# Chunked attention and two feed-forward layers on one core: the first four attention tiles with whole exponentials, a maximum subtracted on TensorE, and a normalisation on GpSimd

## The chip, the core and the metric

The kernel runs on one core of one Trainium2 chip. The metric is device time in microseconds (us) of one execution. Engines are named as the profile names them: PE (TensorE; PEld is its loading of weights), DVE (VectorE), ACT (ScalarE), POOL (GpSimd) and SP (SyncE, here the engine that issues all transfers; SPq is its queue).

## The reference, cut to what matters

```python
def _attn_ref(q, k, v, mem_k, mem_v):        # (4, 8, 768, 64), 8 memory keys
    chunk, left_ctx, right_ctx = (32, 16, 8)
    scale = 1.0 / np.sqrt(D)
    for c in range(S // chunk):
        ...
        scores = scale * np.matmul(q_c, k_full.transpose(0, 1, 3, 2))
        scores = scores - np.max(scores, axis=-1, keepdims=True)
        a = np.exp(scores)
        a = a / (np.sum(a, axis=-1, keepdims=True) + 1e-09)
        out[:, :, c_start:c_end] = np.matmul(a, v_full)
...
h = x @ w_in                                 # x: 3072 tokens x 512; w_in 512 x 2048
g = np.maximum(h, 0.0) + alpha * np.minimum(h, 0.0)
x = g @ w_out                                # layer 1
...
h = x @ w_in2; sp = np.log1p(np.exp(h))      # sp with a cut at 20
out = (h * np.tanh(sp)) @ w_out2             # layer 2
```

Each chunk of 32 queries sees 64 keys: 16 to its left, its own 32, 8 to its right and 8 memory keys. The result, 3072 tokens of 512 numbers, goes through two feed-forward layers. The weights come as float64.

## The kernel before, in words

The tokens are cut into 24 attention tiles of 128 tokens (`T`, 0 to 23) and six blocks of 512 tokens. Layer 1 goes through w1_in in 16 tiles of 128 columns (`j`), each followed by the product with the w1_out tile of the same number. Every float32 operand is split into a high and a low part (`xh`, `xl`, `wi`, `wo`, `gh`, `gl`), and a product is three matmuls: high by high, high by low, low by high.

Nothing runs in the order in which it is written. Every step is given to `Plan.add` (line 108) with its engine, a planned duration, the buffers that it reads and writes, and for some a due time. `Plan.run` (line 132) then sorts the steps of each engine by due times that it works back from the order of PE's steps, which is the written one, and emits each engine's instructions in that order. On the chip each engine takes its instructions strictly one after another. While PE would have nothing to do at the start, the planner puts in matmuls on a tile of zeros, `busy` (line 1758).

The change touches the first block, tiles 0 to 3 (`T0` is 4), and the first weights:

- `load_qk` (line 612) loads keys and queries of a tile. The queries are then copied by ACT and DVE (`place`, line 638) into a tile `qbd` in which each head's half of the rows is zero outside its own columns, so that one matmul serves two heads. POOL fills the zeros (line 584).
- `load_v` (line 676) loads the values, two rows of 2 KB in each of 96 partitions.
- `gate` (line 604) is a transfer of 4 bytes that reads a tile which has just been loaded or scaled. SP issues transfers in order, so what stands behind a gate is held until that tile is ready. There are five: after the keys of tile 3, the values of tiles 0 and 2, and the scaling of the first two w1_in tiles.
- `scores_of` (line 716) makes a tile's scores, 16 matmuls into one bank of PSUM. `rest` (line 774) adds the softmax: for tiles 0 and 1 a maximum (DVE), eight exponentials with their sums (`exps`, ACT, line 755) and a normalisation (DVE, line 772); for tiles 2 and 3 (`WHOLE`) the maximum is subtracted (DVE, `less`, line 762), one exponential covers the tile (ACT, line 765), and DVE sums (line 768).
- `turn_pe` (line 959) transposes the probabilities on PE in two banks, which ACT or DVE copy out; `values_of` (line 793) multiplies them with the values, and ACT and DVE split the result into `xh` and `xl`.
- `load_raw` (line 332) and `to_f32` (line 352) load a weight tile and make float32 of float64: ACT scales the upper words (line 365), DVE puts the bits together (lines 368 and 371); `split_w` (line 402) splits the result (ACT 404, DVE 407).
- `gemm1` (line 1197) is the product with one tile of w1_in. For the first block, tiles 0 and 1 of w1_in are multiplied in two halves of 256 tokens (line 1795). Their banks are 4 and 5 by turns (line 1200), so the product with the third tile writes the bank that `act1` (line 1226) reads for the first: two ACT reads, lines 1229 and 1230.

The order of the first block's steps on PE is one string (line 1073; s scores, t transposes, v values):

```python
first = "s0 s1 t0 s2 t1 s3 v0 t2 v1 t3 v2 v3"
```

## Time and profile before

| | |
|---|---|
| median of 3 runs | 1034.07 us (1033.57 to 1034.28) |
| the profiled execution: its time | 1034.0 us |
| its span, first to last instruction | 1032.1 us |
| mean granted TensorE clock | 0.998 |
| PE busy | 1020.7 us, 99% of the span |
| PEld busy | 842.1 us, 82% |
| DVE busy | 834.1 us, 81% |
| ACT busy | 641.8 us, 62% |
| POOL busy | 6.9 us, 1% |
| DMA | 242.35 MB, 235 GB/s on average |

The span runs from the first to the last instruction of the core; the execution's own time holds 1.9 us more. Busy times are sums over the whole span, and PE's is modelled, as its matmuls overlap. The chain of waits follows the work that ended last back to its start. Durations of one instruction overlap too: an instruction of DVE with 0.68 us may be followed by the next after 0.60.

### The profile page before, as it was taken

What the parts mean: (1) busy time and instruction counts of PE and PEld (TensorE: products, weight loads), DVE (VectorE), ACT (ScalarE), POOL (GpSimd) and SP (SyncE); (2) the same over time, 40 slices, a digit from 0 to 9 for tenths busy, and PEclk for the clock granted to TensorE, in tenths of its full rate; (3) what the DMA queues carried; (4) which work ended last, traced back from release to release, by engine and by line L of the source; (5) the groups of instructions that cost most, each with busy time, mean ns of one, the idle gap of its engine ahead of it and who ended that gap; (6) DMA issues with size and microseconds to landing.
All of it is one profiled execution on the core that took longest, in us unless ns stands there. A gap on an engine that the chain in (4) does not pass through costs nothing.

```text
span 1032.1 us, 19612 instructions
## 1 busy us (share of the span) xinstructions
PE 1020.7 (99%) x7195; PEld 842.1 (82%) x7197; DVE 834.1 (81%) x1481; ACT 641.8 (62%) x1401; POOL 6.9 (1%) x20
## 2 busy tenths in 40 slices
PE   8999999999999999999999999999999999999997
PEld 6888888888888788888888888888888888888886
DVE  7877688888878889999999969697578777578784
ACT  6899756656665655797977657564444744444630
POOL 2000000000000000000000000000000000000000
PEclk9999999999999999999999999999999999999999
DMA  8977785875687773734878899886778766668766
GB/s 254 318 249 241 245 286 168 258 252 177 223 265 268 243 243 123 255 113 165 296 243 292 296 319 322 306 259 193 227 233 261 218 194 193 192 193 262 209 193 146
DMA packets 133929, 242.35 MB, mean 235 GB/s; under 512 B 12874, under 2 KB 50250, under 8 KB 133834
## 3 DMA queue, kind: packets, MB, share of 16 engines
q1 hardware_dynamic: 131658, 240.05, 73.6%
q10 hardware_dynamic: 2176, 1.05, 0.5%
q8 instruction: 57, 0.93, 0.4%
q14 instruction: 38, 0.31, 0.1%
HBM read 182.33 MB, written 58.72 MB: 234 GB/s over the span
## 4 chain that ended last, share of the span: by engine, by line
PE 97%; DMA 1%; ACT 0%; SPq 0%; issue 0%; DVE 0%; ACTq 0%
PE bank L1522 29%; PE bank L1364 22%; PE bank L1259 17%; PE bank L1210 17%; PE bank L1701 7%; PE bank L927 2%; PE bank L861 1%; DMA wo<-in_w_out_dram 1%; PE bank L1494 1%; DMA wo<-in_kw_dram 1%; PE bank L1758 0%; PE bank L805 0%; PE bank L738 0%; PE bank L998 0%; SPq L635 0%
## 5 line engine op out<-in xcount | busy, mean ns | idle before, releaser
L1210 PE MATMUL bank<-xh,wi 128*128 128x512 f32 (+1 forms) x528 | 170.1, 385 | 0.9 <-ACT rstrip L1230 0.9
L1259 PE MATMUL bank<-gh,wo 128*128 128x512 f32 x512 | 170.3, 392 | 0.2 <-issue 0.2
L1210 PEld LDWEIGHTS bank<-xh,wi 128*128 128x128 f32 x528 | 98.2, 188 | 20.7 <-ACT rstrip L1230 1.1
L1259 PEld LDWEIGHTS bank<-gh,wo 128*128 128x128 f32 x512 | 96.0, 188 | 20.6
L1364 PE MATMUL bank<-wo,wo 128*128 128x512 f32 x438 | 111.1, 389 | 0.0
L1210 PE MATMUL bank<-xl,wi 128*128 128x512 f32 (+1 forms) x264 | 101.1, 383 | 0.0
L1259 PE MATMUL bank<-gl,wo 128*128 128x512 f32 x256 | 99.7, 390 | 0.0
L1364 PEld LDWEIGHTS bank<-wo,wo 128*128 128x128 f32 x438 | 82.2, 188 | 17.0
L1522 PE MATMUL bank<-wi,wo 128*128 128x512 f32 x294 | 73.6, 389 | 0.0
L1229 ACT ACTIVATE rstrip<-bank 128x512 f32<-128x512 f32 x64 | 40.7, 636 | 50.7 <-PE bank L1210 50.4
L1364 PE MATMUL bank<-wo,wi 128*128 128x512 f32 x282 | 71.2, 389 | 0.0
L1522 PEld LDWEIGHTS bank<-wi,wo 128*128 128x128 f32 x294 | 55.2, 188 | 11.4
L1522 PE MATMUL bank<-wi,wi 128*128 128x512 f32 x258 | 64.5, 389 | 0.0
L1222 ACT CAST gh<-rstrip 128x512 fp32r<-128x512 f32 x64 | 42.5, 663 | 35.4 <-PE bank L1259 20.4
L1233 DVE SCALAR_TENSOR_TENSOR rstrip<-rstrip,nalpha 128x512 f32<-128x512 f32 x64 | 47.9, 749 | 19.6 <-ACT rstrip L1230 19.1
L1364 PEld LDWEIGHTS bank<-wo,wi 128*128 128x128 f32 x282 | 52.9, 188 | 11.0
L1223 DVE TENSOR_TENSOR gl<-rstrip,gh 128x512 fp32r<-128x512 f32 x64 | 44.2, 690 | 19.6 <-ACT gh L1222 18.8
L1522 PE MATMUL bank<-gh,wo 128*128 128x512 f32 x228 | 58.0, 389 | 0.0
L1015 DVE STREAM_TRANSPOSE aT<-s 32x256 f32<-32x256 f32 x128 | 55.7, 435 | 2.5
L1210 PEld LDWEIGHTS bank<-xl,wi 128*128 128x128 f32 x264 | 49.6, 188 | 9.4
L1522 PEld LDWEIGHTS bank<-wi,wi 128*128 128x128 f32 x258 | 48.4, 188 | 10.0
L1259 PEld LDWEIGHTS bank<-gl,wo 128*128 128x128 f32 x256 | 48.1, 188 | 10.1 <-issue 0.5
(354 smaller groups left out, 2181.7 us busy)
## 6 DMA issues: line engine op xcount, KB each, us to landing
wo<-w2i SPq DMA_DIRECT2D x102, 256.0 KB, 3.0
wo<-w2o SPq DMA_DIRECT2D x100, 256.0 KB, 3.7
wi<-w2o SPq DMA_DIRECT2D x68, 256.0 KB, 3.3
wi<-w2i SPq DMA_DIRECT2D x66, 256.0 KB, 3.1
wo<-in_w_out_dram SPq DMA_DIRECT2D x24, 512.0 KB, 6.8
w2i<-wo SPq DMA_DIRECT2D x24, 512.0 KB, 3.2
w2o<-wo SPq DMA_DIRECT2D x24, 512.0 KB, 3.2
wo<-w1o SPq DMA_DIRECT2D x22, 512.0 KB, 4.8
```

What stands on the lines that cost most here:

```text
L861: nc.tensor.matmul(ps(z)[row : row + CH, i, 2 * a + e, :], qview()[half, 2 * a + z, e].rearrange("p (x c) -> p x c", c=2)[:, :, c], keys(2 ...
L927: nc.tensor.matmul(out[h * 64 : (h + 1) * 64, i, p, c], value(half, c, 2 * p + h), aT()[half, i, (p % 2) * (NP // 2) + p // 2, c, h ^ (p % ...
L1015: nc.vector.transpose(dst[:, :, m // 2, m % 2], src[:, :, keys])
L1210: nc.tensor.matmul(bk.t[:, lo:hi], a, b, start=kk == 0 and i == 0, stop=kk == KT - 1 and i == 2)
L1222: add("act", a_(n), lambda: nc.scalar.copy(g.t[0], src.t[0]), [src], [(g, "h")], at=at)
L1223: add("dve", d_(n), lambda: nc.vector.tensor_sub(g.t[1], src.t[0], g.t[0].bitcast(F32)), [src, (g, "h")], [(g, "l")], at=at)
L1229: add("act", a_(n) - 0.05, lambda: nc.scalar.activation(m.t[0], h.t[:, :n], AF.Relu, scale=-1.0), [h], [m], at=at)
L1233: lambda: nc.vector.scalar_tensor_tensor(r.t[0], m.t[0], nalpha[:, j : j + 1], r.t[0], ALU.mult, ALU.add),
L1259: nc.tensor.matmul(bk.t[:, :n], lt, rh, start=j == 0 and i == 0, stop=j == NJ - 1 and i == 2)
L1364: nc.tensor.matmul(bk.t, l, r, start=start and kk == n == 0, stop=kk == 1 and n == 2, skip_group_check=True,)
L1522: nc.tensor.matmul(bs[db].t, l, r, start=first and k == 0, stop=p == pairs[-1] and k == 2, skip_group_check=True,)
L1701: nc.tensor.matmul(bk.t, l, r, start=start and kk == n == 0, stop=kk == 1 and n == 2, skip_group_check=True,)
```

## The change

The queries of tiles 0 to 3 are no longer placed into `qbd`. Scores read them where they were loaded, with one matmul per head (32 a tile, 64 rows and 32 columns each). Tiles 0 to 3 have one exponential each. For tiles 0 and 1 DVE subtracts the maximum; for tiles 2 and 3 (`ON_PE`) PE does it, by a matmul of the identity with the negated maxima, spread over the columns, that adds to the bank of the scores. DVE sums 66 columns, one of which holds 1e-9. The probabilities of tiles 2 and 3 (`ON_POOL`) are multiplied by the reciprocal sums on POOL. Each of the four tiles has its own buffers for probabilities and their transposes, two of them the former `qbd`, and banks by a table (`EARLY`). The gates are gone. The first loads stand in a fixed order (`first_load`), and the first two w1_in tiles come by one transfer of 1 MB, behind the values of tile 0, into a buffer of the later tokens. The order of the first steps on PE is changed.

```diff
...
-    WHOLE = (2, 3)
...
-    PLAIN = 8
+    ON_POOL = (2,3,)
+    ON_PE = (2,3,)
+    FIRST, PLAIN = 0, 8
...
+    def load_first():
+        raw = Buf(xmakers[1][0])
+        xring.last[1] = [raw]
+        def go():
+            to = raw.t.bitcast(U32).rearrange("p (k f) -> p k f", k=KT)
+            nc.sync.dma_start(to, w1_in[:, : 2 * P].bitcast(U32).rearrange("(k p) f -> p k f", p=P))
+        first_load(P * 8192, go, raw)
+        first_raw.append(raw)
...
     def load_raw(item, **kw_):
         layer, side, j = item
+        if first_raw and item in w1_items[:2]:
+            return first_raw[0]
...
+        two = item in w1_items[:2]
+        def parts_(dtype, n):
+            t = raw.t
+            if two:
+                return t.bitcast(dtype).rearrange("p (k j f w) -> p j k f w", k=KT, j=2, w=n)[:, item[2]]
...
-        if item in w1_items[:2]:
-            gate(raw, 0.0, lambda: words()[1][0:1, 0:1].bitcast(F32))
-        if item in w1_items[:PLAIN]:
...
-    qbd = [own([P, 1024], f"qbd{i}") for i in range(2)] + [spare_slot() for _ in range(2, T0)]
+    qbd = [own([P, 1024], f"qbd{i}") for i in range(2)]
...
-    s_bufs = [own([P, 1024], "s"), spare_slot()]
-    a_bufs = [own([P, 1024], "aT"), spare_slot()]
+    s_bufs = [own([P, 1024], "s"), spare_slot(), *qbd]
+    a_bufs = [own([P, 1024], "aT"), *(spare_slot() for _ in range(1, T0))]
...
     for b in s_bufs:
         for cols in (slice(0, CH), slice(CH + SW, P)):
-            add("pool", 0.6, lambda b=b, cols=cols: nc.gpsimd.memset(wide_of(b)[:, :, cols], 0.0), writes=[b])
-    for b in qbd:
-        for h in range(2):
...
-    stats = ring(ac, [P, 3, 2 * NP], F32, "st", 3)
+            add("pool", 0.31, lambda b=b, cols=cols: nc.gpsimd.memset(wide_of(b)[:, :, cols], 0.0), writes=[b])
+        for rows, col in ((slice(0, 64), CH - 1), (slice(64, P), CH + SW)):
+            add("pool", 0.1, lambda b=b, r=rows, c=col: nc.gpsimd.memset(wide_of(b)[r, :, c : c + 1], 1e-9), writes=[b])
+    stats = ring(ac, [P, 3, 2 * NP], F32, "st", T0)
...
-    def gate(b, when, first=None):
-        n = n_gates[0]
-        n_gates[0] += 1
-        add(
-            "sp", 0.001, lambda: nc.sync.dma_start(gated[:, n : n + 1], first() if first else b.t[0:1, 0:1]), [b],
...
+    EARLY = {"s": ((4,), (5,), (0,), (1,)), "t": ((6, 7), (2, 4), (7, 0), (1, 2)), "v": ((5,), (6,), (7,), (0,))}
+    def att_bank(T, kind, n=0):
+        return bank(EARLY[kind][T][n])
+    n_first = [0]
+    def first_load(size, go, buf):
+        n_first[0] += 1
+        add("sp", size / 330e3, go, writes=[buf], at=n_first[0] - 100.0)
...
-        qt = qbd[T]
+        row = q_rows[T // 2], T % 2
...
-        def qview():
-            return qt.t.rearrange("p (a e h x) -> p a e h x", a=NP, e=2, h=2)
...
-        add("sp", dma_(P * NP * KC * 4), lambda: nc.sync.dma_start(kview(), kw[b, t]), writes=[kt])
-        if T == 3:
-            gate(kt, 12.7)
...
-            def place(eng, h=h):
-                half = slice(h * 64, (h + 1) * 64)
-                copy_on(eng, qview()[half, :, :, h], rows()[half].rearrange("p (a e x) -> p a e x", a=NP, e=2))
...
+        def qview():
+            return rows().rearrange("p (a e x) -> p a e x", a=NP, e=2)
+        first_load(P * 2048, lambda: nc.sync.dma_start(rows(), q[b, t].rearrange("h d a e x -> (h d) (a e x)")), row)
+        first_load(P * NP * KC * 4, lambda: nc.sync.dma_start(kview(), kw[b, t]), kt)
+        kts[T], qs[T] = (kt, kview), (row, qview)
...
-            add("sp", dma_(P * 3520), lambda: nc.sync.dma_start(view(), src), writes=[v])
-            if T in (0, 2):
-                gate(v, 14.7 if T == 0 else 0.0)
+            first_load(W * 4096, lambda: nc.sync.dma_start(view(), src), v)
...
-        sb = s_bufs[T % 2 if T < T0 else 0]
+        (kt, kview), (_, qview) = kts[T], qs[T]
+        bk = att_bank(T, "s")
+        sb = s_bufs[T]
...
-                        nc.tensor.matmul(
-                            ps()[c * 64 : (c + 1) * 64, e * NP + p, :],
-                            qview()[:, p, e].rearrange("p h (x c) -> p (h x) c", c=2)[:, :, c],
-                            kview()[:, p, k0 : k0 + SW],
-                            start=True, stop=True,
-                        )
+                        for h in range(2):
+                            half, lo = slice(h * 64, (h + 1) * 64), c * 64 + h * CH
+                            nc.tensor.matmul(
+                                ps()[lo : lo + CH, e * NP + p, :],
+                                qview()[half, p, e].rearrange("p (x c) -> p x c", c=2)[:, :, c],
+                                kview()[half, p, k0 : k0 + SW],
+                                start=e == p == 0, stop=True, skip_group_check=True,
+                            )
...
-        def exps(g):
-            nc.scalar.activation(
-                s()[:, g, :], ps()[:, g, :], AF.Exp, bias=st.t[:, 0, g : g + 1], scale=0.125,
-                accum_out=st.t[:, 1, g : g + 1],
+        def less():
+            nc.tensor.matmul(
+                bk.t, ident, st.t[:, 0, :].unsqueeze(2).broadcast_to([P, 2 * NP, SW]), start=False, stop=True,
+                skip_group_check=True,
             )
...
+        def less_here():
             nc.vector.tensor_add(s(), ps(), st.t[:, 0, :].unsqueeze(2).broadcast_to([P, 2 * NP, SW]))
         def exp():
-            nc.scalar.activation(s(), s(), AF.Exp, scale=0.125)
+            nc.scalar.activation(s(), ps() if T in ON_PE else s(), AF.Exp, scale=0.125)
...
         def total():
-            nc.vector.tensor_reduce(st.t[:, 1, :], s(), AX.X, ALU.add)
...
-        def norm():
-            nc.vector.tensor_mul(s(), s(), st.t[:, 2, :].unsqueeze(2).broadcast_to([P, 2 * NP, SW]))
+            nc.vector.tensor_reduce(st.t[:, 1, :], wide_of(sb)[:, :, CH - 1 : CH + SW + 1], AX.X, ALU.add)
+        def norm(eng):
+            eng.tensor_mul(s(), s(), st.t[:, 2, :].unsqueeze(2).broadcast_to([P, 2 * NP, SW]))
...
-            if T in WHOLE:
-                add("dve", d_(512), less, [(st, 0), bk], [sb])
-                add("act", a_(512), exp, [], [sb])
-                add("dve", d_(512), total, [sb], [(st, 1)])
+            if T in ON_PE:
+                add("pe", 0.95, less, [(st, 0)], [bk])
             else:
-                add("dve", 0.12, lambda: nc.vector.tensor_scalar_mul(st.t[:, 0, :], st.t[:, 0, :], 0.125), [], [(st, 0)])
-                for g in range(2 * NP):
-                    add("act", 0.29, lambda g=g: exps(g), [(st, 0), bk], [(sb, g), (st, 1, g)])
-            add("dve", 0.12, lambda: nc.vector.tensor_scalar_add(st.t[:, 2, :], st.t[:, 1, :], 1e-9), [(st, 1)], [(st, 2)])
-            add("dve", 0.14, lambda: nc.vector.reciprocal(st.t[:, 2, :], st.t[:, 2, :]), [], [(st, 2)])
-            add("dve", d_(512), norm, [(st, 2)], [sb])
+                add("dve", d_(512), less_here, [(st, 0), bk], [sb])
+            add("act", a_(512), exp, [bk] if T in ON_PE else [], [sb])
+            add("dve", d_(512), total, [sb], [(st, 1)])
+            add("dve", 0.14, lambda: nc.vector.reciprocal(st.t[:, 2, :], st.t[:, 1, :]), [(st, 1)], [(st, 2)])
+            if T in ON_POOL:
+                add("pool", 1.15, lambda: norm(nc.gpsimd), [(st, 2)], [sb])
+            else:
+                add("dve", d_(512), lambda: norm(nc.vector), [(st, 2)], [sb])
...
-        ab = a_bufs[T % 2 if T < T0 else 0]
+        ab = a_bufs[T]
...
-    first = "s0 s1 t0 s2 t1 s3 v0 t2 v1 t3 v2 v3"
+    first = "s0 s1 s2 s3 t0 t1 v0 v1 t2 t3 v2 v3"
...
-    for T in range(T0):
-        load_v(T)
-    for st in block_steps[0]:
+    for go in (partial(load_v, 0), load_first, partial(load_v, 1), partial(load_v, 2), partial(load_v, 3)):
+        go()
+    FIRST_HALF = block_steps[0].index(("v", 3)) + 1
+    for st in block_steps[0][:FIRST_HALF]:
         run_step(st)
```

What these edits move shows on three engines. The names are the program's tiles: `bank` a PSUM bank, `s`, `wo_...` and `qbd` the probabilities, `aT` and `wi_344` their transposes, `vw` and `wi_...` the values.

PE from the scores of tile 3 on (before) and from behind them (now). Before:

```order
L738 MATMUL bank_237<-wo_178,wi_167 64x64 [waits DVE_49,PE_49,DMAHW0_49,Activation_49,Pool_49]
L738 MATMUL bank_237<-wo_178,wi_167 64x64 x15
L974 MATMUL bank_259<-ident,s 96x64 [waits DVE_49]
L974 MATMUL bank_259<-ident,s 96x64 x7
L974 MATMUL bank_270<-ident,s 96x64 x8
L974 MATMUL bank_281<-ident,wo_115 96x64 [waits DVE_49,Activation_49]
L974 MATMUL bank_281<-ident,wo_115 96x64 [waits Activation_49] x7
L974 MATMUL bank_295<-ident,wo_115 96x64 x8
L805 MATMUL bank_306<-aT,vw_207 64x64 [waits DMAHW1_49,Activation_49]
L805 MATMUL bank_306<-aT,vw_207 64x64 x15
```

Now:

```order
L755 MATMUL bank_211<-st_250,ident 128x512 [waits DVE_49,Pool_49]
L972 MATMUL bank_294<-ident,s 96x64 [waits DVE_49,Pool_49]
L972 MATMUL bank_294<-ident,s 96x64 x7
L755 MATMUL bank_256<-st_291,ident 128x512 [waits DVE_49]
L972 MATMUL bank_311<-ident,s 96x64 x8
L972 MATMUL bank_324<-ident,wo_95 96x64 [waits DVE_49,Pool_49]
L972 MATMUL bank_324<-ident,wo_95 96x64 x7
L972 MATMUL bank_335<-ident,wo_95 96x64 [waits PE_49]
L972 MATMUL bank_335<-ident,wo_95 96x64 x7
L803 MATMUL bank_347<-aT,vw_208 64x64 [waits DMAHW0_49,DVE_49,Activation_49]
L803 MATMUL bank_347<-aT,vw_208 64x64 x15
L803 MATMUL bank_370<-wi_344,wi_306 64x64 [waits DMAHW2_49,Activation_49]
```

PE now has two matmuls of 128x512 among the transposes, and a product with values follows the transposes of two tiles as before; the first row of the second such product is the last one shown.

SP from the keys of tile 3 on. Before:

```order
L626 DMA wo_178<-in_kw_dram 128x672 [waits DMAHW0_49]
L682 DMA vw_207<-in_vw_dram 96x2x512 [waits DMAHW1_49]
L682 DMA wi_223<-in_vw_dram 96x2x512 [waits DMAHW2_49]
L340 DMA wi_254<-in_w_in_dram 128x4x256 [waits DMAHW3_49]
L608 DMA gated<-wo_178 1x1 [waits DMAHW4_49,DMAHW0_49]
L340 DMA wi_291<-in_w_in_dram 128x4x256 [waits DMAHW5_49]
L608 DMA gated<-vw_207 1x1 [waits DMAHW6_49,DMAHW1_49]
L682 DMA wi_328<-in_vw_dram 96x2x512 [waits DMAHW7_49]
L608 DMA gated<-wi_254 1x1 [waits DMAHW3_49,Activation_49]
L682 DMA wi_358<-in_vw_dram 96x2x512
L608 DMA gated<-wi_291 1x1 [waits DMAHW5_49,DMAHW2_49,Activation_49]
L340 DMA wi_382<-in_w_in_dram 128x4x256
```

Now:

```order
L644 DMA wo_199<-in_kw_dram 128x672
L684 DMA vw_208<-in_vw_dram 96x2x512 [waits DMAHW0_49]
L341 DMA xh_246<-in_w_in_dram 128x4x512 [waits DMAHW1_49]
L684 DMA wi_306<-in_vw_dram 96x2x512 [waits DMAHW2_49]
L684 DMA wi_322<-in_vw_dram 96x2x512 [waits DMAHW3_49]
L684 DMA wi_364<-in_vw_dram 96x2x512 [waits DMAHW4_49]
L1759 DMA nalpha<-in_alpha_dram 128x16 [waits DMAHW5_49]
L356 DMA wi_391<-in_w_in_dram 128x4x256 [waits DMAHW6_49]
L361 DMA wo_441<-in_w_out_dram 128x1024 [waits DMAHW7_49]
L356 DMA wi_486<-in_w_in_dram 128x4x256 [waits DMAHW0_49]
```

The four-byte transfers to `gated` are gone, and the values of tile 1 now stand behind the 1-MB load to `xh_246`. A row's `DMAHW` wait is for an earlier transfer, the eighth before it.

ACT from its start. Before:

```order
L277 COPY qbd_97<-wo_88 64x8x64 [waits DMAHW0_49]
L756 ACTIVATE s,st_148<-bank_117,st_148 128x64 [waits DVE_49,PE_49]
L756 ACTIVATE s,st_148<-bank_117,st_148 128x64 x7
L756 ACTIVATE wo_115,st_184<-bank_150,st_184 128x64 [waits DVE_49,PE_49]
L756 ACTIVATE wo_115,st_184<-bank_150,st_184 128x64 x7
L277 COPY aT<-bank_259 96x16x32 [waits PE_49]
L277 COPY aT<-bank_270 96x16x32 [waits PE_49]
L277 COPY wi_304<-bank_281 96x16x32 [waits PE_49]
```

Now:

```order
L764 ACTIVATE s<-s 128x8x64 [waits DVE_49]
L764 ACTIVATE wo_95<-wo_95 128x8x64 [waits DVE_49]
L764 ACTIVATE qbd_107<-bank_211 128x8x64 [waits PE_49]
L276 COPY aT<-bank_294 96x16x32 [waits PE_49]
L764 ACTIVATE qbd_110<-bank_256 128x8x64 [waits PE_49]
L276 COPY wi_344<-bank_324 96x16x32 [waits PE_49]
L276 COPY wi_344<-bank_335 96x16x32 [waits PE_49]
L395 ACTIVATE xh_246<-xh_246 128x4x128 [waits DMAHW1_49]
L395 ACTIVATE xh_246<-xh_246 128x4x128
```

Sixteen exponentials of 64 columns are now two of 512, and ACT's first scaling of weights still follows the copies of the first two tiles' transposes.

## Rows read from the trace of the kernel before

**Rows 1.** Page: chain that ended last, shares by engine
```profile
PE 97%; DMA 1%; ACT 0%; SPq 0%; issue 0%; DVE 0%; ACTq 0%
```

**Rows 2.** Chain in order of time, first 50 us: start us, us, what
```profile
13.07 1.12 PE bank L738 x30
...
15.93 1.15 PE bank L805 x32
...
20.89 5.95 DMA wo<-in_w_out_dram
...
29.93 0.50 ACT rstrip L1230
...
30.47 3.02 PE bank L1210 x12
...
36.21 1.50 PE bank L861 x96
```

**Rows 3.** Waits of PE, whole span: us in total, times, longest us
```profile
PE bank L861 <- issue: 1.1, 1, 1.1
PE bank L1210 <- ACT rstrip L1230: 0.9, 1, 0.9
```

**Rows 4.** Timeline of SP: start us, us, engine, line, transfer
```profile
5.02 0.50 SPq L682 DMA_DIRECT2D vw<-in_vw_dram  x1
...
11.30 0.29 SPq L608 DMA_DIRECT2D gated<-wo  x1
11.64 0.40 SPq L340 DMA_DIRECT2D wi<-in_w_in_dram  x1
```

**Rows 5.** Transfers issued at 5.02 and 11.64 us: count, KB, us to landing
```profile
vw<-in_vw_dram SPq DMA_DIRECT2D x1, 384.0 KB, 7.8
...
wi<-in_w_in_dram SPq DMA_DIRECT2D x1, 512.0 KB, 6.5
```

**Rows 6.** Stretches: busy us of PE, PEld, DVE, ACT, POOL; clock, DMA share, GB/s
```profile
10.00:14.00 4.00, 4.00 (x73) 2.75 (x72) 2.99 (x11) 3.51 (x24) 0.00 (x0) 1.00 1.07 249
...
26.00:32.00 6.00, 5.14 (x38) 4.68 (x37) 4.41 (x8) 4.36 (x9) 0.00 (x0) 1.00 1.03 375
```

**Rows 7.** ACT by form, 0 to 31 us: busy us, mean ns, idle before
```profile
L756 ACT ACTIVATE s<-bank,st 128x64 f32<-128x64 f32 x8 | 2.4, 324 | 4.7 <-DVE st L783 4.7
...
L766 ACT ACTIVATE s<-s 128x512 f32<-128x512 f32 x1 | 0.6, 644 | 0.0
```

**Rows 8.** Timeline of DVE: start us, us
```profile
15.20 0.68 DVE L763 TENSOR_TENSOR s<-bank,st 128x512 f32<-128x512 f32 x1
15.79 0.68 DVE L763 TENSOR_TENSOR wo<-bank,st 128x512 f32<-128x512 f32 x1
```

**Rows 9.** PE: scores by form, then timeline of transposes and half-products
```profile
L738 PE MATMUL bank<-wo,wo 128*64 128x64 f32 x32 | 1.2, 227 | 0.0
...
14.12 0.86 PE L974 MATMUL bank<-ident,s 64*96 64x64 f32 x15
...
23.59 0.39 PE L1210 MATMUL bank<-xh,wi 128*128 128x256 f32 x1
...
29.33 0.28 PE L1210 MATMUL bank<-xh,wi 128*128 128x256 f32 x1
...
54.10 1.03 PE L998 MATMUL bank<-ident,s 128*128 128x128 f32 x8
```

**Rows 10.** POOL by form, whole span: busy us, mean ns, idle before
```profile
L584 POOL MEMSET wo<- 64x512 f32 x2 | 1.0, 518 | 0.1
L579 POOL MEMSET wo<- 128x256 f32 x2 | 0.6, 310 | 0.1
...
L1762 POOL TENSOR_SCALAR nalpha<-nalpha 128x16 f32<-128x16 f32 x1 | 0.5, 525 | 1.1 <-DMA nalpha<-in_alpha_dram 1.1
masks.py:199 POOL TENSOR_SCALAR_AFFINE_SELECT ident<-ident 128x128 f32<-128x128 f32 x1 | 0.3, 293 | 0.0
...
L285 POOL MEMSET floors<- 128x1 f32 x1 | 0.1, 98 | 0.3 <-POOLq L1947 0.3
```

81 lines of the change are left out of this document (33 added, 48 removed).

## The prediction

> **What bounds the kernel now.** I read the chain of waits first, then its first 50 us in order of time, then PE's waits, the loads (their queue, their landings, the rates), and last the durations by form. The chain is PE for 97% of the span [rows 1]. PE's named waits after 30 us are one of 1.1 us and scraps [rows 3], so the remaining 1000 us are matmuls back to back and no part of the change reduces them. What can change is when that unbroken run starts. I take as its start the first product that has all 512 tokens, the product of the third 128 columns of w1_in ("j2"), at 30.47 us [rows 2]. Before it, the first two products ran as four half-products from 23.59 to 29.61 without a gap, 1.5 us each [rows 9]. Then PE waited 0.9 us for ACT [rows 3]: j2 reuses j0's bank, and ACT's two reads of it ended at 30.43, because ACT had stood behind the load of w_out's first tile, which landed at 26.84 [rows 2]. So two things put j2 at 30.47: attention of tiles 0 to 3 ended at 23.6, and a weight load that was sent late held ACT.
>
> The profiled execution took 1034.0 us with a span of 1032.1, so 1.9 us lie around the span. The median of the runs is 1034.07, and I let 1034.0 stand for it. 0.2% is 2.07 us, about what a measurement of this kernel can tell from no change. I call the loads of queries, keys and values of tile T q, k and v with its number, and w the new 1-MB load that fetches the first two tiles of w1_in at once.
>
> **The change part by part.**
>
> *Exponentials.* Tiles 0 and 1 spent 8 ACTIVATEs each (0.32 us apiece for tile 0), every one with an accumulator read. One whole exponential takes 0.64 [rows 7]. DVE pays for that with a subtraction and a sum per tile, 0.6 us each in steady succession (15.20, then 15.79) [rows 8], and saves seven placements of q. Both engines are idle often enough before 12 us, where loads rule, so I cost this at nothing. The cover is k3's load: tile 3's scores cannot begin before it lands.
>
> *Scores.* No q is placed, so scores wait for loads alone. k3 landed at 11.26: the small transfer that waits for it went out at 11.30 [rows 4]. The eight loads of q and k stand first in both kernels. alpha's 8 KB leave that stretch, so I take 11.2. In place of 16 matmuls in 1.2 us [rows 2, 9] a tile has 32 on 64 rows and 32 columns. The late attention issues 64 of that shape in 1.50 us [rows 2], so 0.75 us. The scores of tile 3 then run from 11.2 to 11.95, where before they began at 13 [rows 2].
>
> *PE's subtraction.* Two matmuls of 128x512 in f32 stand on PE's path. Lower end: two passes of 512 columns at 0.21 us, the pace of the half-products (1.5 us for 12 of 256 columns [rows 9]), 0.43. The nearest row is the f32 transpose: eight of 128 columns in 1.03 us [rows 9]. A transpose leaves one record and a product two (32 for the 16 scores matmuls [rows 9]), so 512 columns cost 4 x 2 x 0.11 = 0.9. Upper end: twice that, 1.8. I take 0.95.
>
> *The order of PE.* After tile 3's scores PE runs subtraction, t0, subtraction, t0, t1, t1, v0, v1, t2, t3, v2, v3 (t: transposes, two banks per tile; v: products with the values). One bank of transposes takes 0.4 (a tile's two in 0.86 [rows 9]), one v product 1.15 [rows 2]. 11.95 + 0.95 + 0.4 + 0.95 + 3 x 0.4 = 15.45. v0 follows at 15.5 and ends at 16.65. Then PE needs v1.
>
> *The loads.* The gates go, so loads stream in order: k3, v0, w, v1, v2, v3, then weights. SP holds eight in flight, each later one waiting for the eighth before it, which has long landed where it matters. v1 now stands behind 1.05 MB of w. v0 landed at 12.8 (5.02 + 7.8 [rows 4, 5]). Lower end for v1: the 1.44 MB of w and v1 at the 375 GB/s of 26 to 32 us [rows 6], 3.85 us, so 16.7. Upper end: at the 249 GB/s of 10 to 14 us [rows 6], 5.8 us, so 18.6. The nearest row is the second w_in load of before, the last of the same bytes (q, k, v0, v1 and two w_in tiles), which landed at 11.64 + 6.5 = 18.1 [rows 5]. It was sent late, behind a gate, and came in pieces half as long as w's, so I take 17.8, a little earlier.
>
> The Trainium skill ("DMA: Bandwidth & Descriptors", section on queues, rings and completion order) says that one transfer is split over rings of independent engines, and lands only when the slowest is done. The trace agrees as far as it shows this: from 10 to 14 us the DMA engines were full (share 1.07) at 249 GB/s [rows 6], and a load of 0.5 MB took 6.5 us to land [rows 5]. By strict order at the full rate v1 would come at 16.7 and the sum would be that of rival A.
>
> *From v1 to j2.* v1 runs 17.8 to 18.9, the four transposes to 20.5, v2 and v3 to 22.85 (20.6 + 2 x 1.12). ACT and DVE need 0.5 and 0.6 us per 512-column step [rows 2, 8]. DVE's last work for the first half-product ends at about 22.95: t2's second bank is there at 19.85, and five steps follow (two copies, the low word of w's second tile, v1's remainder, w's first remainder). Its result is needed by the third matmul, so DVE just keeps pace. The half-products run 22.85 to 28.75 less some overlap at the seam, 28.65. ACT's two reads of j0's bank can end at 28.55 if the weights allow (next point). So j2 starts at 28.65 and not at 30.47: **1.8 us earlier**, 0.75 from attention and 1.05 from the wait that goes.
>
> *Weights.* After v1 I add, at 1.4 us for 0.39 MB and 1.5 for 0.52 MB: v2 19.2, v3 20.6, the third w_in tile 22.2, w_out's first 23.7, the fourth w_in tile 25.2. ACT's order puts the scaling of that fourth tile ahead of its two reads of j0's bank, 2.3 us before j2 can start. It binds beyond 26.3, so the margin is 1.1 us (four more ACT steps of 0.5 to 0.6 lie between).
>
> *GpSimd.* Two multiplies of 128x512 by a broadcast reciprocal. The sums of tiles 2 and 3 are ready at about 14.6 and 16.2. The trace has no two-tensor GpSimd operation. Lower end: a memset of 512 columns, 0.52. Nearest: the one that reads and writes 128x128 takes 0.29, less 0.1 of start (a one-column memset takes that) 1.5 ns a column, so 0.9, and with a second operand to read 1.5. Upper end: the small multiply of 128x16 takes 0.53 [rows 10]; if all of that over 0.1 were per column, 512 columns would be 13.7. I take 1.5, which ends them at 16.1 and 17.7, before PE reaches t2 at 18.9 and t3 at 19.7: hidden by v1's wait, and if v1 came early, 0.3 on the path.
>
> The Trainium skill ("GPSIMD Engine Reference", section on elementwise cycle accounting) has a two-tensor operation at 1.96 times DVE's time. DVE's took 0.68 here, so an estimate by that page is 1.35; the sum would stay as it is, and rival C would be out.
>
> *The rest.* Eight memsets of 0.31 and eight of one column at 0.1 [rows 10] end on GpSimd before 6, and the first sum needs them near 9. Two q loads for tiles 4 and 5 now wait for t2 and t3 in the SP queue (19 to 20.5); v3's own slot holds them until 20.6 anyway. The planner writes DVE, ACT and SP in a somewhat different order later, with the same work, and PE's order stays until late in the first product layer. I cost that at nothing, with 0.3 us either way; its cover is PE's gapless run, which the engines beside it have fed so far.
>
> Sum: 1034.0 - 1.8 = **1032.2 us**. The granted clock was 1.00 in the stretches read [rows 6], the level of 2.4 GHz; I take it unchanged.
>
> **The rivals.**
>
> A. *No wait for v1.* It lands by 16.7, and PE's own sequence from k3 on is the limit. PE would be through v1 at 17.8 and not 18.9; 0.9 of these 1.1 us reach the half-products, since DVE's steps on w are then the limit. They start at 21.95, j2 at 27.75, a gain of 2.7 us: 1031.3. With cheaper subtractions it could reach 1030.8. For it: 375 GB/s later in the run. Against: 249 GB/s just when v loads are in flight.
>
> B. *Weights late in the ungated stream.* The fourth w_in tile ends 4.2 MB behind k3, and one straggling load moves it. If it lands at 28.2, j2 is at 30.5 and the gain is nil: 1034.0. Landing at 26.9, or v1 at 18.6, still leaves 1.2 or 1.0. For it: w_out's first load took 6 us to land in an emptier queue [rows 2].
>
> C. *GpSimd's multiply takes over the path (slower).* t2 and t3 wait for two multiplies in a row, so j2 moves by 14.6 + 2n - 19.7 with n the time of one. It passes the 1.8 gained at n = 3.5 us and is 2.07 slower than before at n = 4.5. At 6 us: 1039.1. A single delay d ahead of the first multiply does the same: the second then ends at 17.7 + d, j2 moves by d - 2.0, and it decides from d = 3.8. I give the slow multiply 0.05 and the single delay 0.03. For it: 0.53 us for 16 columns. Against: 0.29 for 128.
>
> The Trainium skill ("GPSIMD Engine Reference", section on instruction dispatch) speaks against the change in one way: the first call to freshly loaded GpSimd code costs about 6 us more. By that rule the second multiply would end near 23.7 and the time would be 1036.2. No GpSimd row of before shows such a gap ahead of a first use [rows 10].
>
> **How the numbers follow.** Forecast (v1 waited for, landing between 17.1 and 18.6, gain 1.0 to 2.4): 0.50. A: 0.27. B: 0.15. C: 0.08. Faster by over 0.2%, that is under 1032.0: all of A and a third of the forecast's case, 0.43. Slower by over 0.2%: three quarters of C and a little of B, 0.08. Within 0.2%: 0.49. The range of 1030.8 to 1034.3 holds A with its cheap subtractions, the forecast and most of B, and leaves out C and the worst of B.
>
> **What would show it right or wrong.** Right: tile 3's scores near 11.2, PE idle about a microsecond before v1 with a DMA as what ended it, the first half-product near 22.9, j2 near 28.7, and 36.21's burst of late scores [rows 2] near 34.4. Subtractions on PE of 0.9 to 1.0 each and multiplies on GpSimd of 1 to 2. Wrong: a wait of PE on GpSimd before t2 or t3 (C), j2 held by ACT behind a w_in load (B), or new waits on PE after 35 us, which would mean that the planner's new order gives back what the start gained.

## The result, and the profile after

The changed kernel took 1044.68 us (median of 6 runs, 1041.96 to 1045.09), the kernel before 1034.25 beside it (median of 6, 1033.57 to 1037.43). The ratio is 1.0091, with a 95% interval of 1.0075 to 1.0107: **slower by 0.9%**, where 1032.2 us and no measurable change had been forecast. The profiled execution took 1045.09 us, its span is 1043.3. PE was busy for 1028.6 us and not 1020.7, at a mean granted clock of 0.992 and not 0.998. The chain of waits, which had 97% of PE before [rows 1], has now, by engine:

```profile
PE 89%; DVE 5%; DMA 3%; issue 1%; ACT 1%; SPq 0%; DVEq 0%; ACTq 0%
```

Lines have moved by a few: 740 holds the scores, 755 PE's subtraction, 803 the v products, 972 the transposes, 1208 and 1257 the products, 1699 a later group of products (in the experiments up to 9 further on).

The time goes in two places. The first is the start. PE's timeline, with the idle time ahead of a row and what ended it in brackets:

```profile
9.22 1.10 PE L740 MATMUL bank<-wo,wi 64*32 64x64 f32 x64
...
11.75 0.42 PE L740 MATMUL bank<-wo,wi 64*32 64x64 f32 x12 [0.46 <-DMA wo<-in_kw_dram]
15.08 0.97 PE L740 MATMUL bank<-wo,wi 64*32 64x64 f32 x52 [2.92 <-issue]
15.99 1.66 PE L755 MATMUL bank<-st,ident 128*128 128x512 f32 x2
...
22.53 1.97 PE L803 MATMUL bank<-aT,vw 96*64 96x64 f32 x32
...
30.22 1.10 PE L803 MATMUL bank<-wi,wi 96*64 96x64 f32 x32
31.25 0.39 PE L1208 MATMUL bank<-xh,wi 128*128 128x256 f32 x1
```

The scores of tile 3 start at 11.75, as soon as their keys are there, stop after 12 of 64 records, and go on 2.92 us later. Nothing that the profile shows ended this pause ("issue"). Behind it everything is slow: a v product takes 1.97 us where it had 1.15 [rows 2], until the last one at 30.22. The first half-product stands at 31.25 and not at 23.59 [rows 9]. By stretch (behind the stretch its length, then busy us of PE, PEld, DVE, ACT and POOL; the last three figures are granted clock, DMA share and GB/s):

```profile
8.00:12.00 4.00, 3.54 (x107) 1.99 (x96) 3.67 (x8) 1.26 (x2) 0.00 (x0) 1.00 1.06 290
12.00:16.00 4.00, 1.08 (x64) 0.83 (x53) 0.29 (x1) 0.00 (x0) 0.00 (x0) 1.00 1.05 289
16.00:30.00 14.00, 14.00 (x163) 10.66 (x162) 8.68 (x16) 7.19 (x13) 2.48 (x3) 0.52 0.92 258
30.00:40.00 10.00, 10.00 (x103) 9.41 (x101) 9.12 (x17) 7.96 (x15) 0.00 (x0) 0.99 1.00 328
```

PE was busy for 1.08 of the 4 us from 12 to 16, and from 16 to 30 the clock is 0.52, which is the level of 1.2 GHz, where before it was 1.00 [rows 6]. The DMA engines are full throughout.

The second place is far behind. I counted PE's product matmuls in order and compared the start of the one that the kernel before runs at 240 us: 6.5 us late. The same at 540 us: 11.0 late, and so to the end. So 4.5 us more are lost between, nearly all from 310 to 520 us. PE's waits between the two points add up to 3.6 us, against 1.3 in the kernel before; the other 2 us are steps of PE that follow each other more slowly, and no wait shows them. In that stretch the chain leaves PE (start us, us, what):

```profile
320.38 0.70 DVE wo L490
...
321.10 0.33 SPq L495
...
322.81 5.24 DMA wo<-w1o
...
328.19 0.93 PE bank L1257 x3
```

A w1_out tile that has to be read back (`wo<-w1o`) stood in SP's queue behind a store that waited for DVE, and PE waited for it. At 377 us PE waited 0.7 us by issue, and from 420 to 520 us it waits in small pieces for ACT and DVE in a later group of products (0.4, 0.4, 0.3 and 0.3 us at line 1699). Before, PE waited for nothing from 420 to 520 us.

What the forecast had small was small. The two multiplies on POOL:

```profile
19.51 1.04 POOL L770 TENSOR_TENSOR qbd<-qbd,st 128x512 f32<-128x512 f32 x1 [15.29 <-DVE st L782]
23.40 1.04 POOL L770 TENSOR_TENSOR qbd<-qbd,st 128x512 f32<-128x512 f32 x1 [2.85 <-DVE st L782]
```

The transposes that need them began at 26.14. And the 0.9 us that PE waited for ACT before the third product [rows 3] are gone, as forecast.

### The profile page after: what moved, and what is told of

It is laid out like the page before. It is cut to its first block, busy times and chain, and to the rows that moved or that the text cites. A ratio compares the mean times of both kernels' runs of the same rounds, so it can differ in the third digit from the quotient of the medians.

```text
span 1043.3 us, 19774 instructions
## 1 busy us (share of the span) xinstructions
PE 1028.6 (99%) x7317; PEld 846.1 (81%) x7317; DVE 833.0 (80%) x1471; ACT 636.3 (61%) x1367; POOL 5.9 (1%) x26
## 3 DMA queue, kind: packets, MB, share of 16 engines
q10 hardware_dynamic: 2176, 1.05, 0.5%
## 4 chain that ended last, share of the span: by engine, by line
PE 89%; DVE 5%; DMA 3%; issue 1%; ACT 1%; SPq 0%; DVEq 0%; ACTq 0%
PE bank L1520 28%; PE bank L1362 22%; PE bank L1208 16%; PE bank L1257 16%; PE bank L925 2%; PE bank L1699 2%; PE bank L859 1%; DMA wo<-in_kw_dram 1%; DVE wo L490 1%; DMA raw<-in_w_out_dram 1%; PE bank L803 1%; DVE b L1670 1%; PE bank L1492 1%; DMA wo<-in_w_out_dram 1%; PE bank L972 1%
## 5 line engine op out<-in xcount | busy, mean ns | idle before, releaser
L1520 PEld LDWEIGHTS bank<-wi,wo 128*128 128x128 f32 x294 | 55.2, 188 | 11.5
L1231 DVE SCALAR_TENSOR_TENSOR rstrip<-rstrip,nalpha 128x512 f32<-128x512 f32 x64 | 47.9, 748 | 13.7 <-ACT rstrip L1228 12.7
L1520 PEld LDWEIGHTS bank<-wi,wi 128*128 128x128 f32 x258 | 48.3, 188 | 10.6 <-DVE wi L1452 0.6
```

The lines of the kernel that those rows point to most:

```text
L1231: lambda: nc.vector.scalar_tensor_tensor(r.t[0], m.t[0], nalpha[:, j : j + 1], r.t[0], ALU.mult, ALU.add),
L1520: nc.tensor.matmul(bs[db].t, l, r, start=first and k == 0, stop=p == pairs[-1] and k == 2, skip_group_check=True,)
```

## The experiments

My theory of the start was that PE had run out of fetched instructions, and that the fetch, a packet of 16 KB in the queue of kind "instruction", stood behind the loads, which nothing holds any more. Of the later loss I thought that the planner's order had made it. The table has the runs and, from their profiles, three times in us: the start of the first half-product (23.59 in the kernel before), how late the product comes that the kernel before runs at 240 us, and what is lost behind it up to the last product. These three are of one execution each, and executions of one kernel differ: e2's four went from 1046.6 to 1052.6 us, and its profile is of the slowest; e10's is of its fastest (1040.2).

```text
run                    median us  ratio [95%]               first   late at  lost
                                                            half    240 us   later
changed kernel         1044.68    1.0091 [1.0075, 1.0107]   31.25    6.5      4.5
e1_pause_k3            1041.86    1.0083 [1.0056, 1.0110]   29.36    5.1      3.4
e2_16_tiny             1048.75    1.0144 [1.0116, 1.0172]   28.70    4.0     14.5
e3_after_now           1042.37    1.0076 [1.0059, 1.0092]   30.41    5.8      2.2
e4_before_now          1034.46    1.0003 [0.9991, 1.0014]   23.59    0.9      0.1
e5_pause_v1_first      1043.92    1.0087 [1.0072, 1.0102]   28.86    5.4      4.0
e6_before_no_gates     1035.92    1.0016 [1.0004, 1.0028]   24.46   -0.1      1.3
e7_reload_sent_early   1054.97    1.0198 [1.0173, 1.0222]   30.95    7.0     17.1
e8_pause_dve_norm      1043.08    1.0084 [1.0067, 1.0101]   27.28    2.5      5.2
e9_after_lead          1038.18    1.0045 [1.0031, 1.0058]   28.21    4.0      0.4
e10_before_less_lead   1042.32    1.0082 [1.0070, 1.0095]   23.11   -1.3      7.6
e11_two_pauses_lead    1037.05    1.0031 [1.0019, 1.0043]   27.56    4.0     -0.7
e12_v1_first_lead      1039.69    1.0050 [1.0033, 1.0068]   27.22    4.1      1.2
e13_halves_lead        1041.99    1.0060 [1.0043, 1.0077]   29.76    6.0      3.0
e14_second_half_last   1042.13    1.0069 [1.0054, 1.0084]   28.12    7.6      1.4
e15_halves_own_tiles   1039.05    1.0047 [1.0033, 1.0060]   26.01    3.5      1.4
```

### The pause in the scores (e1, e2, e6)

**e1.** A hold behind the keys of tile 3:

```diff
+    def pause(n, buf):
+        n_first[0] += 1
+        add("sp", 0.001, lambda: nc.sync.dma_start(gated[:, n : n + 1], buf.t[0:1, 0:1]), at=n_first[0] - 100.0)
...
+        if T == 3:
+            pause(0, kt)
```

> The changed kernel with one addition: a transfer of 4 bytes that reads the keys of tile 3, directly behind their load, so that values and weights are sent only when those keys have landed; the order on PE, DVE and ACT is that of the changed kernel. Theory 1 (TensorE ran out of fetched instructions at 12.17 us, and the fetch, one 16-KB packet, had to get through a full load stream): k3 lands by 10.5 instead of 11.6, PE's idle time put down to issue falls from 2.9 us to under 1, the granted clock stays at 1.00 from 7 us on, the first half-product starts at 23.5 to 25 instead of 31.24, and the time is 1037 to 1039, since 4 to 5 us that were lost after 250 us stay lost. Theory 2 (the pause belongs to PE's own program, whatever the loads do): 2.5 to 3.5 us of issue stay inside the scores of tile 3, the clock falls behind it, and the time is 1043 to 1046.

PE's timeline:

```profile
11.69 1.10 PE L748 MATMUL bank<-wo,wi 64*32 64x64 f32 x64
...
16.89 1.15 PE L811 MATMUL bank<-aT,vw 96*64 96x64 f32 x32 [0.28 <-issue]
21.45 1.97 PE L811 MATMUL bank<-wi,wi 96*64 96x64 f32 x32 [3.41 <-DMA wi<-in_vw_dram]
...
29.36 0.58 PE L1216 MATMUL bank<-xh,wi 128*128 128x256 f32 x1
```

The scores of tile 3 ran through, and work up to v0 kept the full clock. So theory 1 was right on the pause, but its start and its time were a miss. With the loads held to 10.7 us, v1 landed at 21.3, PE waited 3.41 us for it, and the half clock came behind this wait instead.

**e2.** Sixteen more matmuls at PE's start:

```diff
+    for _ in range(16):
+        add("pe", 0.0, lambda: nc.tensor.matmul(idle.t[:16, :16], busy[:, :16], busy[:, :16], start=True, stop=True))
```

> The changed kernel with 16 matmuls of 16x16 more at PE's start, 32 instructions, nothing else moved. Theory 1 (PE stops where a block of its instruction stream ends, by my count behind 443 instructions, 12 records into the scores of tile 3): the pause moves by 32 instructions to the four filling matmuls behind tile 2's scores, near 10.3; the scores of tile 3 then run without a break from 13 to 13.7, 1.4 to 2 us earlier than before they ended, and the time falls by 1 to 2.5 us to 1042 to 1043.5. Rival (the second part of k3 arrives late and the profile doesn't show that wait): the pause stays behind 12 records of tile 3's scores and the time is that of the changed kernel within 1 us.

```profile
10.61 0.39 PE L1756 MATMUL bank<-busy 128*128 128x512 bf16 x1
14.54 1.46 PE L1756 MATMUL bank<-busy 128*128 128x512 bf16 x3 [3.54 <-issue]
15.93 1.93 PE L740 MATMUL bank<-wo,wi 64*32 64x64 f32 x64
```

The pause moved to the place counted: it comes behind 444 records of PE (weight loads and matmuls), in the changed kernel behind 443 (34 of filling matmuls with 2 records each, 384 of the scores of three tiles with 4 each, 25 of tile 3's). So it is a seam in the instruction stream and nothing that tile 3 does. In this run it cost 3.54 us (2.6 to 3.5 in the four runs that keep the changed kernel's first loads), the clock was at half for 3.4 us, and the first half-product came at 28.70. The time was a miss, by the later loss (below).

The fetch itself, in the changed kernel from 8.4 to 12.3 us, then from 12.3 to 12.6 (queue, kind: packets, MB, share of 16 engines):

```profile
q1 hardware_dynamic: 534, 1.07, 105.6%
q8 instruction: 1, 0.02, 24.6%
```

and in e1 from 8.4 to 9.0:

```profile
q1 hardware_dynamic: 64, 0.13, 56.4%
q8 instruction: 1, 0.02, 11.2%
```

In the eight runs with a hold behind k3 that packet starts at 8.6 to 9.2 us, behind 275 to 290 records of PE. In the kernels without it PE passes its 277th record at about the same time (8.3 in the changed kernel), but the packet starts at 11.5 to 12.8, when PE has already run dry. It took 1.2 us here, and PE went on 1.5 us behind its end. In the four other kernels with the changed order and no hold that gap is 1.3 to 1.5 us, and 1.4 to 1.5 again at later seams of e6 and e15. The trace doesn't name the engine that a packet is for; that it is PE's is my reading of these times. In the kernel before PE's 277th record was at 13.6, the packet at 14.1, and the seam, near the 430th record, cost 0.25 us at 17.3:

```profile
17.33 1.23 PE L805 MATMUL bank<-wi,wi 96*64 96x64 f32 x32 [0.25 <-issue]
```

The Trainium skill ("Runtime: NRT & Kernel Launch", section on instruction fetch mechanics) says that an engine's instructions come in blocks of 16 KB, 256 at a time, the next block fetched while the current one runs, and that crossing a block is mostly hidden. The traces agree on the size: packets of 16 KB, and seams some 250 records apart (behind 443 in the changed kernel, 692 and 943 in e15). Of the cost the measurement decides: 2.9 us.

**e6.** The kernel before without its gates:

```diff
     def gate(b, when, first=None):
+        return
```

> The kernel before with its five 4-byte transfers left out and nothing else: PE, DVE and ACT have the order of before, the loads stream without a hold. Theory 1 (PE's instruction stream has a seam near its 440th instruction, here between the products of v0 and v1, and what it costs is set by the load stream): PE's idle time by issue there grows from 0.25 us to 1.5 to 3.5, the clock falls behind it, and the time is 1035 to 1041. Rival (the seam cost 2.9 us only because of the changed kernel's own order of instructions): issue stays under 0.6 there, weights come earlier, and the time is 1032.5 to 1034.5.

```profile
16.70 1.15 PE L806 MATMUL bank<-wi,wi 96*64 96x64 f32 x32 [0.25 <-issue]
...
24.20 0.34 PE L806 MATMUL bank<-wi,wi 96*64 96x64 f32 x4 [0.91 <-issue]
```

My theory as worded was wrong: the seam by v1 still cost 0.25 us and the clock held. The next seam, behind 689 records, grew to 0.91 us, and the start came out level (its 1035.9 us are in the theory's range, but by a later loss of 1.3 us, most of it waits by issue at 295 and 369 us). Free loads alone don't make the pause, and neither does the changed PE order alone (e1). It takes both together: four tiles of scores with 128 records each and not 64, one behind the other, so that PE reached the seam at 12 us and not at 17.

### The later loss (e3, e4, e7, e9, e10)

**e3, e4.** The planner's clock moved by 0.7 us behind the first half-products, back in the changed kernel (shown) and, with `plan.now += 0.7`, forward in the one before.

```diff
     first_products(1)
+    plan.now += -0.7
```

> The changed kernel with 0.7 us taken off the planner's clock behind the first half-products, which undoes the shift of its due times; up to there nothing moves, later the steps of all engines come in another order. Theory 1 (the 4.7 us lost after 250 us come from the order that the planner happened to make): the burst of late scores stays at 42.8 within 0.3, and the time moves by more than 1 us against the changed kernel's 1044.7, to 1039 to 1043 if the new order is as good as before's. Rival (the later loss follows from the late start, by transfers and other engines that had been planned for an earlier PE): 1043.7 to 1045.7.

> The kernel before with 0.7 us added to the planner's clock behind the first half-products; the first 30 us are untouched. If the later order is worth microseconds by chance, the time moves off 1034.2 by more than 1 us, to 1036 to 1039 if it falls as badly as in the changed kernel. If the order is worth nothing and the later loss has another cause: 1034.2 within 0.7 us.

The changed kernel's later loss fell from 4.5 to 2.2 us, as theory 1 had it (its start, of the same order, came 0.7 us earlier). Executions of the changed kernel are 3.1 us apart, so this step alone shows little. The kernel before lost nothing that can be measured, where I had thought of a microsecond or more.

**e7.** The reloads of w1_out tiles emitted earlier:

```diff
+            if i in self.early:
+                start[i] = max([start[d] + self.tasks[d][1] for d in self.tasks[i][3]] + [start[i] - 14.0])
```

> The changed kernel with the reloads of w1_out tiles sent up to 14 us earlier in SP's queue, ahead of stores and loads that they stood behind; PE, DVE and ACT keep the changed kernel's order. Theory (part of the later loss is SP's queue: at 321 us a reload stands behind a store that waits for DVE, and lands when PE already waits for it): PE's waits for wo from w1o in 300 to 340 us (1.4 us, and 0.7 of issue behind it) go, the loss between 300 and 345 us shrinks by 0.8 to 2 us, and the time is 1042 to 1044, if the stretch of 420 to 520 us is as before. Rival (DVE is behind anyway, and the next step is late by as much): under 0.5 us, 1044 to 1045.5.

A plain miss: 10 us slower than the changed kernel. PE's wait for the reload went, and these came between 300 and 420 us (us in total, times, longest):

```profile
PE bank L929 <- DVE aT L1017: 2.6, 2, 1.4
PE bank L929 <- DMA qbd<-in_vw_dram: 2.0, 2, 1.7
PE bank L1261 <- DVE gl L1225: 1.4, 1, 1.4
```

With each of two groups of these waits the granted clock went to 1.2 GHz for 6.8 us (from 332.9 and from 377.3), and 12 of the 17 us are lost between 310 and 420 us, where both lie. My reading is that what was put first held up the values of the late attention, and that the queue as a whole was late, not one transfer in it; no run shows this by itself.

**e9, e10.** Evaluating the planner gave a reason. It places the steps of ACT, DVE, POOL and SP by due times counted back from PE's, and PE's own steps then come out later than these, by 10.6 us in the kernel before and by 7.4 in the changed one, as the products are planned 3.2 us earlier against their due times. My theory was that this lead is what the other engines live on. The edits are `plan.now += -3.2` in the changed kernel and `plan.now += 3.2` in the one before.

> The changed kernel with 3.2 us taken off the planner's clock behind the first half-products; up to there nothing moves. In the planner's own schedule PE's steps run 10.6 us behind their due times in the kernel before and 7.4 us in the changed one: the other engines, whose steps are placed by due times, had been given 3.2 us less lead, and that schedule has waits of PE of 2.4 us in all behind 300 us, where the one of before has none. With 3.2 us taken off, the lead is 10.7 again, and the later order is within 60 rows of before's on PE. Theory (the loss after 250 us is lost lead): the burst of late scores stays at 42.2 to 43, no loss behind 250 us over 1 us, time 1039 to 1041.5. Rival (the loss comes from the late start or from the changed buffers): 1042.5 to 1045.5.

> The kernel before with 3.2 us added to the planner's clock behind the first half-products; the first 30 us are untouched, and the later order is within 46 rows of the changed kernel's on PE. Theory (lost lead): a loss of 2.5 to 5 us between 250 and 520 us, the start as before, time 1036.5 to 1039.5. Rival (before's buffers and loads bear any order): 1033.5 to 1035.5.

Both went the theory's way, and both times fell outside its range. With the lead back the changed kernel loses 0.4 us later and not 4.5. It also started 2.5 us earlier, which the edit doesn't touch (below): of the 6.5 us between e9 and the changed kernel that part is luck. The kernel before, with its instructions up to the first half-products untouched, loses 7.6 when the lead is taken from it, more than I had expected. Of that, 2.2 us are a wait by issue in a burst of late scores at 371 us (1.1 in the kernel before), and behind it the clock was at 1.2 GHz for 3.4 us. So the change of order is shown to cost this much; that it does so by late engines alone is not. DVE's busy time (third figure, of 50 us) and PE's (first) in two stretches of e9:

```profile
350.00:400.00 50.00, 50.00 (x579) 41.39 (x578) 44.30 (x87) 25.76 (x72) 0.00 (x0) 1.00 0.74 230
400.00:450.00 50.00, 49.03 (x215) 39.58 (x214) 48.31 (x78) 35.58 (x60) 0.00 (x0) 1.00 0.53 181
```

and of the changed kernel and, last, the kernel before:

```profile
350.00:400.00 50.00, 49.31 (x575) 40.50 (x574) 42.53 (x88) 30.05 (x97) 0.00 (x0) 1.00 0.80 252
400.00:450.00 50.00, 49.27 (x216) 39.80 (x215) 47.89 (x75) 31.42 (x52) 0.00 (x0) 1.00 0.53 169
...
400.00:450.00 50.00, 50.00 (x221) 40.83 (x220) 49.41 (x82) 37.70 (x66) 0.00 (x0) 1.00 0.56 191
```

From 400 to 450 us DVE is busy for 48 to 49 of 50 us, so what it has not done before 400 it can hardly catch up. From 350 to 400 it had done 1.8 us less in the changed kernel.

e9 also prices the half clock. Its first 30 us have the changed kernel's order and the same pause (3.27 us), but the clock recovered earlier:

```profile
16.00:20.00 4.00, 4.00 (x32) 1.79 (x25) 2.40 (x5) 1.45 (x3) 0.10 (x1) 0.80 1.08 220
20.00:30.00 10.00, 8.32 (x192) 7.62 (x189) 9.05 (x16) 8.08 (x15) 2.38 (x3) 1.00 1.03 334
```

From the end of the pause to the first half-product it took 13.6 us (14.63 to 28.21), the changed kernel 16.2 (15.08 to 31.25): some 2.6 us of the changed kernel's start hang on the clock. As e9 too was at half clock for 3.4 us, the whole price of the clock may be higher.

### Can the changed start be mended? (e5, e8, e11 to e15)

All these have the hold behind k3. **e5** sends v1 ahead of the 1-MB load; **e8** also has DVE multiply.

```diff
-    for go in (partial(load_v, 0), load_first, partial(load_v, 1), partial(load_v, 2), partial(load_v, 3)):
+    for go in (partial(load_v, 0), partial(load_v, 1), load_first, partial(load_v, 2), partial(load_v, 3)):
...
-    ON_POOL = (2,3,)
+    ON_POOL = ()
```

> As the run with the pause behind the keys of tile 3, and in addition the values of tile 1 are sent ahead of the 1-MB weight load. That run had no pause of PE in the scores, but PE then waited 3.41 us for v1 behind that load, and the clock fell to 1.2 GHz behind this wait. Theory 1 (any long standstill of PE costs twice, by its length and by the half clock behind it): v1 lands by 17, PE has no wait over 1.2 us before the products, the granted clock stays 1.00 from 7 us on, the first half-product starts between 22 and 23.8 (23.59 before, 31.24 in the changed kernel), and the time is 1035 to 1039, as 3 to 5 us of loss after 250 us remain. If the half clock came from the new instructions themselves, PE's clock would fall without a long wait, half-products would start behind 26, and the time would be over 1040.

> As the run with the pause and the values of tile 1 first, but DVE and not GpSimd multiplies the probabilities of tiles 2 and 3. If GpSimd's multiply is hidden, as forecast (1.04 us each in the changed kernel), the first half-product starts within 0.4 us of that run's, and the time differs by what the later order makes, up to 2.5 us either way. If GpSimd is on the path of the transposes of tiles 2 and 3, the first half-product starts 0.5 to 1.5 us earlier here; if DVE is, later.

e5 missed: the 1-MB load landed at 21.8, 9.6 us behind its issue, and ACT, whose order has its scaling ahead of the copies of t2 and t3, stood until then. PE's wait, and what ACT waited for:

```profile
25.24 1.98 PE L811 MATMUL bank<-wo,wi 96*64 96x64 f32 x32 [4.33 <-DVE wo L276]
```

```profile
21.82 1.21 ACT L395 ACTIVATE xh<-xh 128x512 f32<-128x512 f32 x2 [4.14 <-DMA xh<-in_w_in_dram]
```

e8 doesn't settle what it was made for: its scores of tile 3 started 0.7 us earlier, as the loads came in, and its half clock was shorter, and either is too much beside a multiply of 1.04 us. e5's own rows answer it: the second multiply ended at 19.06, and the transposes began at 19.45 without a wait.

**e11** to **e15** also have the lead back. **e11** and **e12** have a second hold that waits for the 1-MB load; in e12 v1 is ahead of that load. **e13** takes the two weight tiles in two loads of 512 KB, **e14** puts the second one behind v3, **e15** gives each a buffer of its own. What e11, e13 and e15 add (e15's lines against e13):

```diff
-    for go in (partial(load_v, 0), load_first, partial(load_v, 1), partial(load_v, 2), partial(load_v, 3)):
+    for go in (partial(load_v, 0), load_first, partial(load_v, 1), lambda: pause(1, first_raw[0]), partial(load_v, 2), partial(load_v, 3)):
...
+            to = raw.t.bitcast(U32).rearrange("p (k f) -> p k f", k=KT)[:, :, j * 2 * P : (j + 1) * 2 * P]
...
-        raw = first_raw[0]
+        raw = Buf(xmakers[1][j])
```

> The changed kernel with three repairs: a 4-byte transfer behind the keys of tile 3 that holds the loads (as in the first run with a pause), a second one behind the values of tile 1 that waits for the 1-MB weight load, so that the values of tiles 2 and 3 and the weights behind them don't share its time, and the 3.2 us off the planner's clock. Theory (the start was lost to the seam in PE's instruction stream, to loads that land late, and to the half clock that follows any long wait; the rest to lost lead): no pause by issue in tile 3's scores, the 1-MB load lands before 18, v1 before 19, no wait of PE over 1.5 us behind 12 us, clock 1.00 throughout, first half-product at 22.9 to 24.5, no loss after 250 us, time 1032 to 1035. Rival (the pauses cost as much as they save): a wait of 2 to 4 us for v1 or v2, half clock behind it, first half-product behind 26, time 1036 to 1040.

> As the run with two pauses and the restored lead, but with the values of tile 1 ahead of the 1-MB load, and 3.0 us off the planner's clock instead of 3.2 (the planner's schedule then has no wait of PE, with a lead of 10.6). In that run PE waited 1.66 us for v1, the clock fell, and the first half-product came at 27.6. Theory (with the seam, the lead and the late loads all mended, the forecast's own steps hold): v1 lands by 16.5, the 1-MB load by 18.5, no wait of PE over 1.2 us between 12 us and the first half-product, clock 1.00 from 7 us on, first half-product at 23 to 24.5, the burst of late scores at 34.7 to 36.5, time 1032 to 1034.5. Rival (t2 and t3 are held by ACT behind the scaling of the 1-MB load, as when v1 was first sent ahead): a wait of 2 to 4 us before v2, half clock behind it, first half-product behind 26, time 1036 to 1038.

> The changed kernel with the pause behind the keys of tile 3, the first two weight tiles in two loads of 512 KB (order v0, v1, first tile, v2, second tile, v3), the pause counted as 3 us by the planner, so that ACT's scaling stands behind copies that are ready earlier, and 2.0 us off the planner's clock (lead 10.7, no planned wait). The 1-MB load landed 6.6 to 8.4 us behind its issue in the last two runs, with little beside it. Theory (the start's last loss is this load, with ACT's queue behind it): the first half lands by 18, no wait of PE over 1.5 us between 12 us and the first half-product, that at 23 to 25, no loss behind 250 us, time 1032 to 1035. Rival (any load order with a pause is some microseconds late): a wait of 2 to 4 us, half clock behind it, time 1036 to 1039.

> As the run with the weight tiles in two loads, but with the values of tile 3 ahead of the second weight tile. Theory: v3 no longer binds, the second tile is needed 1.5 us later than the first, so the first half-product starts within 0.7 us of that run's, time within 1 us of it. Rival: the second tile comes late and the second half-product waits 1 to 2 us for it.

> As the first run with the weight tiles in two loads, but each into a buffer of its own. In that run the two shared one buffer, and ACT's scaling of the first, which had landed at 18.8, also waited for the second, at 22.4: its wait of 4.2 us was of my making. Theory (with seam and lead mended, the start hangs on when ACT gets the first weight tile): scaling at 18.5 to 19.5, no wait of PE over 1.5 us behind 12 us, first half-product at 22.8 to 24.8, no loss over 1 us behind 250 us, time 1032.5 to 1035.5. Rival (the pause makes the weights too late in any shape): first half-product behind 25.5, time 1036 to 1039.

None of them beats the kernel before: e11, e12, e13 and e15 came out in the range of their rivals or above, and e14's first half-product 1.6 us earlier than e13's, where I had expected 0.7 at most (its time was within 1 us of e13's, as expected). Each wait of PE over 1.5 us that began between 17 and 25 us was for values that landed late (e11 1.66 us for v1, e12 3.98 for v2), or for ACT behind a weight load (e13 4.24, e14 3.35; part of both is my own, as steps on the first tile waited for both loads). e15 is the only one without such a wait, and its clock stayed at 1.00 up to the first half-product; but PE stopped at its second and third seam (0.9 and 1.5 us):

```profile
PE bank L811 <- issue: 1.2, 2, 0.9
PE bank L1764 <- issue: 1.7, 2, 1.5
```

The first half-product came at 26.0, 2.4 us behind before's. The second seam did not move it: PE reached v3 at 23.33 just behind its values, which landed at 23.20, so the load was the limit there. The third seam stood right ahead of the first half-product. PE was through v3 at 24.5, and the low word of the first weight tile was ready at 24.62 on DVE, so without that seam the first half-product could have begun near 24.6: an estimate from these rows, and still 1 us behind before's. A version with fewer PE instructions there and the other parts kept was not tried.

## Why the prediction was wrong, step by step

- *Scores, 11.2 to 11.95.* They started at 11.75 and need 1.10 us, not 0.75. Off by 0.9 us together, in size alone.
- *The order of PE: 11.95 + 0.95 + ... = 15.45.* **This step failed.** It let PE run whenever its data were there. PE stood for 2.92 us at a seam. The profile before showed such waits by "issue", 0.25 us in the products of v1 and 1.1 us in a burst of late scores [rows 3]; I passed over the first, took the second as a single event, and didn't ask what they would cost with twice the instructions in a full load stream.
- *The subtraction.* 1.06 us from one start to the next step in e1, for 0.95: right.
- *"The granted clock ... I take it unchanged."* **This failed too**, as a consequence: 0.52 from 16 to 30 us. Seam and clock are the two parts of the start's loss, 2.9 and some 2.6 us. Of the 8.4 between 31.25 and the 22.85 of the forecast the scores are another 0.9; the remaining 2 us I didn't take apart.
- *Loads.* v1 landed at 18.9 (17.8 forecast, 18.6 the upper end), the third w_in tile at 23.6 (22.2), the fourth at 26.3 (25.2). All a microsecond or a little more late; none of it bound, because PE was later still.
- *From v1 to j2.* The 1.05 us of ACT's wait went as forecast: late by 7.7 us at the first half-product, by 6.6 at the third product. (22.85 and four half-products of 1.5 us make 28.85, where the forecast has 28.75: 0.1 us, no matter here.)
- *GpSimd.* 1.04 us each for 1.5, hidden: right. (The forecast's 1.35 is 1.33, 1.96 times 0.68, and was too high as well.) Rival C and its first-call delay didn't come: the first multiply began 0.2 us behind the reciprocal (19.32). The Trainium skill ("GPSIMD Engine Reference", section on instruction dispatch) has some 6 us for that; this trace doesn't show them.
- *The rest: "I cost that at nothing, with 0.3 us either way."* **The third failure**, 4.5 us. The cover that I named, PE's gapless run fed by engines beside it, was real but thin: DVE had 0.6 us to spare in 50 from 400 to 450 us in the kernel before, and what keeps it ahead, by e9 and the planner's own numbers, is the lead, of which the change took 3.2 us. How late engines, seams and clock share this loss is open in part. I had named "new waits on PE after 35 us" as what would show this wrong; that is what came.
